# A margin of planned time on what TensorE waits for, in a kernel whose order of work a list scheduler writes

## The chip, the cores and the metric

The kernel runs on one NeuronCore of a Trainium2 chip. The metric is the device time of one execution in microseconds; lower is better. Work is done by TensorE (matrix products into PSUM), VectorE (DVE), ScalarE (ACT) and GpSimd (POOL); SyncE (SP) issues all transfers. Each engine runs its own instructions in the order in which the program gives them and waits on semaphores for the others.

## The reference

Two independent branches on inputs of 2048 x 448, with their results side by side in an output of 2048 x 896.

```python
def _A_ref(x, dft_seq_re, dft_seq_im, dft_hid_re, dft_hid_im):
    a = jnp.einsum("bsd,ed->bse", x, dft_hid_re)
    b = jnp.einsum("bsd,ed->bse", x, dft_hid_im)
    return jnp.einsum("ts,bse->bte", dft_seq_re, a) - jnp.einsum("ts,bse->bte", dft_seq_im, b)

def _B_ref(x, wqkv, wo):
    B, S, D = x.shape            # 1, 2048, 448
    H = 16; Dh = D // H          # 28
    ...
    scores = jnp.einsum("bhqd,bhkd->bhqk", q, k) * Dh ** -0.5
    p = _softmax(scores, axis=-1)
    o = jnp.einsum("bhqk,bhkd->bhqd", p, v)
    return (lambda x, *d: x.transpose(*d))(o, 0, 2, 1, 3).reshape(B, S, D) @ wo
```

## The kernel before

**Work.** Branch A is a Fourier mixing step: 32 tiles of rows of the hidden transform (`hidden`) and then, for 16 tiles of rows and two parts, real and imaginary, 48 products each against the sequence matrices (`sequence`, L558). Every operand is split into a rounded part and a remainder, and three products make up one (`Piece`: ACT rounds a 256 KB piece of the matrix, POOL or at the start DVE subtracts). Branch B makes q and k (`project`) and v (`values`; L458 with `hidden`), then runs attention for 64 units, that is 16 heads and four chunks of 512 queries, and last multiplies by the output matrix (L853).

**Two kinds of unit.** `unit_kept`, three of a head's four chunks, computes 16 score products of 128 keys x 512 queries (L702). ACT, for the second one ACT or DVE, copies each out of its bank (L335, L337) and DVE takes a running maximum in the tile `rm` (L709, L712). Then come four transpositions (L719), a reduction (L721), four transpositions (L728), the subtraction of the maximum on POOL or DVE (L745) and the exponentials on ACT (L749). `unit_twice`, one chunk of each head, computes the scores once for their maxima (L652, with DVE's L656) and again with the maxima as further rows of the product (L680, with ACT's exponentials L684). Its q rows lie in one of two tiles `qr`, which `load_q` fills (L585, L586) when the unit before last has let the tile go. The product with v is issued in groups of eight (`pv_group`, L633; 16 records of the profile), two groups a unit, and `unit_out` copies the result out on ACT or DVE. `head_out` folds the four partial sums of a head (L763) and divides.

**Fill.** The products of L458 and L558 need few results of the other engines. They are spread over the span as fill: their keys (`fkey`) run from 8 to 1120 on the planner's clock, and they use two PSUM banks of their own (`fill_s`). Attention has the other six (`bank_s`).

**The order** is written by a list scheduler on the host, while the program is built. Each piece of work is a `Task` with a key, the engines that may run it with a duration for each, the tasks that it depends on, and the `Slot`s (tiles or banks from a pool of `Slots`) that it uses. `Schedule.run` steps through time. Whenever an engine is idle it looks through that engine's heap of ready tasks in the order of their keys and takes the first whose slots are to be had (`can_take`) and whose locks are free; what can't be taken is set aside for the next look. A task counts as seen by other engines `lat` after its end (0.15, for TensorE 0.25); then its slots go back to their pool and its dependents are woken. Dependents on the same engine are woken at its end (`own`). The planner's durations are constants: 0.2335 and 0.2365 for a product of 512 columns, 0.2065 for one of 448, 0.60 for a DVE step over a bank with `RAW` = 0.16 more between two maxima on one tile, 0.48 for a copy on ACT. After a value group it takes another value group first, if one can be taken, and it counts `PE_TURN` = 0.22 for each turn from other products to one. The order in which tasks are taken is the order of the instructions of each engine; their semaphore waits follow from what they read and write. On the chip nothing knows of the planner's times.

Of the kernel before, what the change touches and what calls it, by code (L numbers as in the profile page):

```python
# [50 lines left out]
RAW = 0.16  # L51
LANES = 8
FLOW = 200.0
PE_TURN = 0.22


class Slot:


    def __init__(self, pool):  # L60
        self.pool, self.i, self.users, self.lock = pool, None, 0, 0.0
        self.key = None
# [6 lines left out]
class Slots:  # L69


    def __init__(self, tiles, in_turn=False):
        self.tiles, self.in_turn = tiles, in_turn
        self.free = list(range(len(tiles)))
        self.turns = []

    def slot(self):
# [1 line left out]
        self.turns.append(s)  # L79
        return s  # L80

    def can_take(self, slots):
        n = len(self.free)
        if n < len(slots):
            return False
        if self.in_turn:
            return all(s in self.turns[:n] for s in slots)
        return True

    def take(self, slot):  # L90
        slot.i = self.free.pop(0)
        self.turns.remove(slot)


class Task:
    __slots__ = ("engs", "key", "emit", "lat", "use", "lock", "left", "then", "mode", "n", "dmas", "own")


class Schedule:
# [26 lines left out]
            self.wake(t)  # L126
        return t

    def wake(self, t):
        for e in t.engs:  # L130
            heapq.heappush(self.ready[e], (t.key, t.n, t))

    def run(self):
        now, events, count = 0.0, [], 0
        for p in self.pools:
            p.turns.sort(key=lambda s: s.key)
        idle = {e: True for e in self.ENGINES}
        mode = 0
        done = set()
        landed, flow = [], 0.0  # L140
        while True:
            for e in self.ENGINES:
                if not idle[e]:
                    continue
                aside, pick, first = [], None, None
                if e == "SP" and len(landed) >= LANES and landed[-LANES] > now + 1e-9:
                    heapq.heappush(events, (landed[-LANES], 2, count, "tick", None))
                    continue
                heap = self.ready[e]
                while heap:  # L150
                    item = heapq.heappop(heap)
                    t = item[2]
                    if t.n in done:
                        continue
                    wants = {}
                    for s in t.use:
                        if s.i is None:
                            wants.setdefault(s.pool, []).append(s)
                    if any(not p.can_take(w) for p, w in wants.items()) or any(x.lock > now + 1e-9 for x in t.lock):
                        aside.append(item)  # L160
                        continue
                    if e == "PE" and mode == 1 and t.mode == 0 and pick is None:
                        if not any(x[2].mode == 1 and x[2].n not in done for x in heap):
                            pick = t
                            break
                        first = first or item
                        aside.append(item)
                        continue
                    pick = t
                    break  # L170
                if pick is None and first:
                    pick = first[2]
                    aside.remove(first)
                for item in aside:
                    heapq.heappush(heap, item)
                if pick is None:
                    continue
                t = pick
                done.add(t.n)
                for s in t.use:  # L180
                    if s.i is None:
                        s.pool.take(s)
                dur = t.engs[e]
                if e == "PE":
                    if t.mode > mode:
                        dur += PE_TURN
                    mode = t.mode
                lat = t.lat
                if e == "SP":

                    at = now
                    for size, extra in t.dmas:
                        if len(landed) >= LANES:
                            at = max(at, landed[-LANES])
                        flow = max(flow, at + 0.4) + size / FLOW
                        landed.append(max(at + 1.35 + size / 170 + extra, flow + 1.1))
                        at += 0.38
                    dur = at - now
                    lat = max(landed[-len(t.dmas):]) - at + 0.1
                t.emit(e)  # L200
                count += 1
                idle[e] = False
                for x in t.lock:
                    x.lock = now + dur + 0.05
                heapq.heappush(events, (now + dur, 0, t.n, "free", (e, t)))
                heapq.heappush(events, (now + dur + t.own, 1, t.n, "own", (e, t)))
                heapq.heappush(events, (now + dur + lat, 1, t.n, "seen", (e, t)))
                if t.lock:
                    heapq.heappush(events, (now + dur + 0.06, 2, t.n, "tick", None))
            if not events:  # L210
                break
            now = self.now = events[0][0]
            while events and events[0][0] <= now + 1e-9:
                _, _, _, what, x = heapq.heappop(events)
                if what == "free":
                    idle[x[0]] = True
                elif what == "own":
                    for n in x[1].then:
                        if x[0] in n.engs and len(n.engs) == 1:
                            n.left -= 1  # L220
                            if n.left == 0:
                                self.wake(n)
                elif what == "seen":
                    e, t = x
                    for s in t.use:
                        s.users -= 1
                        if s.users == 0:
                            s.pool.free.append(s.i)
                    for n in t.then:
                        if e in n.engs and len(n.engs) == 1:  # L230
                            continue
                        n.left -= 1
                        if n.left == 0:
                            self.wake(n)
        assert count == self.n, (count, self.n, now)
        return now

# [661 lines left out]
```

## Time and profile before

| | |
|---|---|
| median of three runs | 1205.03 us (1199.01 to 1207.03) |
| profiled execution | 1200.74 us |
| its span in the profile | 1199.0 us |
| granted clock of TensorE in it | 0.997 |

The profile's engines are PE (matmuls), PEld (weight loads of TensorE, which overlap matmuls), DVE, ACT, POOL and SP; a "q" behind a name is its sequencer. In lists of waits the columns are: engine, tile and line that waited, `<-` what ended the wait, then the total in us, the number of waits and the longest. "issue" stands for waits that nothing in the profile explains. In a timeline each row has the start, the time it took, engine, line, operation, tiles, shape and how many instructions are merged; in square brackets stands the idle time of the engine before it and what ended it. A gap of TensorE is shown where no matmul's record covers it; since the records of successive matmuls overlap, a late start can be covered. A product with v stands as two records (2,048 for 1,024 instructions).

### The profile page before, as it was taken

How to read it: one execution, taken by the hardware profiler on the slowest of the kernel's cores; microseconds unless marked ns; L12 is line 12 of the kernel's file. 1: busy time of each engine (PE TensorE's matmuls, PEld its weight loads, DVE VectorE, ACT ScalarE, POOL GpSimd, SP SyncE). 2: the span in 40 equal slices, each digit the busy share in tenths (PEclk: the TensorE clock that was granted, in tenths of full speed). 3: DMA queues.
4: the chain of work that ended last, by engine and by line, in shares of the span. 5: the costliest groups of instructions: out<-in, count | busy, mean ns of one | idle time of the engine just before them, and what ended most of it. 6: DMA issues, size and time to landing. Idle time of an engine off the chain costs nothing.

```text
span 1199.0 us, 19665 instructions
## 1 busy us (share of the span) xinstructions
PE 1170.1 (98%) x6404; PEld 795.4 (66%) x6404; DVE 919.5 (77%) x1429; ACT 1055.1 (88%) x1768; POOL 949.2 (79%) x567
## 2 busy tenths in 40 slices
PE   7999999999999999999999999999999999999998
PEld 5876666666667666576666666666567666676588
DVE  6599979888788788787888888888768878867301
ACT  4279999999999999898999999999979999999733
POOL 3157777889989789776988799789869888989963
PEclk9999999999999999999999999999999999999999
DMA  8873244332233231323232333233322323223542
GB/s 255 176 189 110 91 141 144 97 81 75 87 87 92 69 99 58 101 74 104 73 104 66 101 98 98 65 88 90 106 87 73 105 82 108 84 72 98 190 151 107
DMA packets 106150, 125.15 MB, mean 104 GB/s; under 512 B 47460, under 2 KB 61412, under 8 KB 104788
## 3 DMA queue, kind: packets, MB, share of 16 engines
q1 hardware_dynamic: 106048, 123.91, 35.5%
q8 instruction: 50, 0.82, 0.3%
q14 instruction: 52, 0.43, 0.1%
HBM read 89.98 MB, written 33.75 MB: 103 GB/s over the span
## 4 chain that ended last, share of the span: by engine, by line
PE 85%; ACT 4%; DMA 4%; DVE 2%; issue 1%; SPq 1%; POOL 1%; DVEq 0%; POOLq 0%; ACTq 0%
PE bank L558 23%; PE bank L633 17%; PE bank L702 14%; PE bank L458 13%; PE bank L652 5%; PE bank L680 5%; PE bank L853 3%; DMA qr<-qkd 2%; PE bank L719 2%; ACT kept L335 2%; PE bank L728 2%; DVE rm L712 2%; ACT kept L749 1%; PE bank L763 1%; DMA sm<-kept 0%
## 5 line engine op out<-in xcount | busy, mean ns | idle before, releaser
L745 POOL TENSOR_TENSOR kept<-kept,mb 128x1024 f32<-128x1024 f32 x280 | 667.2, 2404 | 76.7 <-ACT mb L730 54.4
L712 DVE TENSOR_TENSOR rm<-bank,rm 128x512 f32<-128x512 f32 x672 | 461.1, 686 | 68.0 <-PE bank L702 21.7
L335 ACT ACTIVATE kept<-bank 128x512 f32<-128x512 f32 (+1 forms) x736 | 414.6, 620 | 63.1 <-PE bank L702 39.0
L749 ACT ACTIVATE kept<-kept 128x1024 f32<-128x1024 f32 x384 | 401.1, 1081 | 13.4 <-POOL kept L745 7.7
L558 PE MATMUL bank<-big,whi 128*128 128x448 f32 x1024 | 324.1, 370 | 0.0
L702 PE MATMUL bank<-qk,k 84*128 84x512 f32 x768 | 292.3, 414 | 1.6 <-DVE rm L712 0.9
L434 POOL TENSOR_TENSOR wlo<-wraw,whi 128x512 fp32r<-128x512 f32 (+1 forms) x166 | 203.7, 1230 | 95.4 <-ACT whi L429 60.1
L633 PE MATMUL bank<-kept,v 128*32 128x512 f32 x2048 | 243.8, 597 | 1.2 <-ACT kept L749 0.8
L558 PEld LDWEIGHTS bank<-big,whi 128*128 128x128 f32 x1024 | 193.2, 190 | 29.5 <-issue 7.5
L656 DVE TENSOR_REDUCE mx<-bank 128x1 f32<-128x512 f32 x256 | 173.5, 683 | 31.4 <-PE bank L652 30.3
L702 PEld LDWEIGHTS bank<-qk,k 84*128 84x128 f32 x768 | 141.5, 189 | 80.6 <-DVE rm L712 22.5
L558 PE MATMUL bank<-big,wlo 128*128 128x448 f32 x512 | 189.1, 369 | 0.4 <-POOL wlo L434 0.4
L684 ACT ACTIVATE kept<-bank 128x512 f32<-128x512 f32 x256 | 155.4, 617 | 4.8 <-PE bank L680 4.3
L633 PEld LDWEIGHTS bank<-kept,v 128*32 128x32 f32 x2048 | 56.0, 109 | 124.4 <-issue 110.1
L745 DVE TENSOR_TENSOR kept<-kept,bank 128x1024 f32<-128x1024 f32 x104 | 125.8, 1212 | 7.0 <-ACT mb L730 6.5
L429 ACT ACTIVATE whi<-wraw 128x512 fp32r<-128x512 f32 x167 | 108.1, 648 | 13.8 <-PE bank L558 6.2
L652 PE MATMUL bank<-k,qr 84*128 84x512 f32 x256 | 104.1, 417 | 12.3 <-DMA qr<-qkd 8.4
L558 PEld LDWEIGHTS bank<-big,wlo 128*128 128x128 f32 x512 | 97.0, 190 | 14.8 <-issue 2.5
L680 PE MATMUL bank<-qr,k 86*128 86x512 f32 x256 | 104.6, 415 | 0.0
L337 DVE COPY kept<-bank 128x512 f32<-128x512 f32 (+1 forms) x48 | 32.7, 682 | 61.9 <-PE bank L702 29.2
L458 PE MATMUL bank<-big,whi 128*128 128x512 f32 x196 | 71.9, 411 | 6.8 <-ACT big L396 5.3
L652 PEld LDWEIGHTS bank<-k,qr 84*128 84x128 f32 x256 | 47.7, 190 | 43.4 <-DVE rm L712 11.3
(80 smaller groups left out, 1065.9 us busy)
## 6 DMA issues: line engine op xcount, KB each, us to landing
wraw<-wre SPq DMA_DIRECT2D x64, 256.0 KB
wraw<-wim SPq DMA_DIRECT2D x64, 256.0 KB
wraw<-xa SPq DMA_DIRECT2D x32, 256.0 KB
out<-kept SPq DMA_DIRECT2D x32, 224.0 KB
k<-qkd SPq DMA_DIRECT2D x15, 448.0 KB
qkd<-kept SPq DMA_DIRECT2D x24, 256.0 KB
qk<-qkd SPq DMA_DIRECT2D x48, 112.0 KB
qkd<-wdh SPq DMA_DIRECT2D x17, 256.0 KB
```

Source lines behind the costliest of these rows:

```text
L335: nc.scalar.activation(dst, src, AF.Copy)
L434: b = sch.add(e, key + 1.5, lambda g: eng[g].tensor_tensor(self.lo.t[:, :n], raw.t[:, :n], f32(self.hi.t)[:, :n], op=ALU.subtract), deps=[ ...
L458: nc.tensor.matmul(o.t[:, :cols], w(), x(), start=(i == 0), stop=(i == n - 1))
L558: nc.tensor.matmul(o.t[:, :D], a.t[:, k, :], b[:, q * 4 + k, :], start=(q == 0 and k == 0 and j == 0), stop=(q == 3 and k == 3 and j == 2))
L633: nc.tensor.matmul(o.t[j * VW:(j + 1) * VW, :], VT[h].t[:, kt // 4, j, :], pairs[i // 2].t[:, i % 2, :], start=(kt < 4), stop=(kt >= NT - 4))
L652: m = pe(key, lambda e, o=o, kc=kc, qt=qt: nc.tensor.matmul(o.t, q.t[:KR, qt * P:(qt + 1) * P], KT[h].t[:KR, kc * CH:(kc + 1) * CH], start ...
L656: ms.append(dve(key - 20, lambda o=o, kc=kc, qt=qt: nc.vector.tensor_reduce(mx.t[:, qt, kc:kc + 1], o.t, axis=AX.X, op=ALU.max), deps=[m], ...
L680: m = pe(key, lambda e, o=o, kt=kt: nc.tensor.matmul(o.t, KT[h].t[:KR + 2, kt * P:(kt + 1) * P], q.t[:KR + 2, :], start=True, stop=True), ...
L702: m = pe(key, lambda e, o=o, kt=kt: nc.tensor.matmul(o.t, KT[h].t[:KR, kt * P:(kt + 1) * P], q.t[:KR, :], start=True, stop=True), deps=[*l ...
L712: prev = dve(key - 20, lambda o=o: nc.vector.tensor_tensor(rm.t, o.t, rm.t, op=ALU.max), deps=[m, prev], use=[rm, o], lock=[o], own=RAW)
L745: eng[e].tensor_tensor(s.t, s.t, over_pair(pm.t if e == "DVE" else mb.t), op=ALU.add)
L749: es.append(act(key, lambda s=s: nc.scalar.activation(s.t, s.t, AF.Exp, scale=SCALE), 0.96, deps=[sh], use=[s]))
```

## The change

The planner takes a task on TensorE only if everything it waits for has been there for 0.15 us of planned time. A pool now keeps with each free tile the time since when it is free, and a task the time at which its last dependency was seen. For tasks on TensorE both must lie at least `AHEAD` = 0.15 before now; for the other engines the margin is zero. A task that is woken by one on its own engine, or has no dependency, has the stamp -1 and passes. Until the margin has passed the planner sees the next ready task in the order of keys, which may be fill. A further event 0.15 after each task has been seen makes the planner look again. No task, duration, key, tile or pool is changed.

```diff
+AHEAD = 0.15
...
-        self.free = list(range(len(tiles)))
+        self.free = [(i, -1.0) for i in range(len(tiles))]
...
-    def can_take(self, slots):
-        n = len(self.free)
+    def can_take(self, slots, before):
+        n = sum(since <= before for _, since in self.free)
         if n < len(slots):
             return False
...
-        slot.i = self.free.pop(0)
+        slot.i = self.free.pop(0)[0]
...
-    def wake(self, t):
+    def wake(self, t, since=-1.0):
+        t.since = since
         for e in t.engs:
             heapq.heappush(self.ready[e], (t.key, t.n, t))
...
                 heap = self.ready[e]
+                before = now - (AHEAD if e == "PE" else 0.0) + 1e-9
                 while heap:
...
-                    if any(not p.can_take(w) for p, w in wants.items()) or any(x.lock > now + 1e-9 for x in t.lock):
+                    if t.since > before or any(not p.can_take(w, before) for p, w in wants.items()) or any(
+                            x.lock > now + 1e-9 for x in t.lock):
                         aside.append(item)
                         continue
...
-                            s.pool.free.append(s.i)
+                            s.pool.free.append((s.i, now))
...
-                            self.wake(n)
+                            self.wake(n, now)
+                    heapq.heappush(events, (now + AHEAD, 2, t.n, "tick", None))
```

More of the change, by code (lines that the diff above doesn't have):

```diff
@@ L90, in take @@
     def take(self, slot):
-        slot.i = self.free.pop(0)
+        slot.i = self.free.pop(0)[0]
         self.turns.remove(slot)
 class Task:
-    __slots__ = ("engs", "key", "emit", "lat", "use", "lock", "left", "then", "mode", "n", "dmas", "own")
+    __slots__ = ("engs", "key", "emit", "lat", "use", "lock", "left", "then", "mode", "n", "dmas", "own", "since")
 class Schedule:
```

## The prediction

> **What bounds the kernel now.** I read the page first: the busy times, then the chain that ended last.
>
> ```profile
> span 1199.0 us, 19665 instructions
> ...
> PE 1170.1 (98%) x6404; PEld 795.4 (66%) x6404; DVE 919.5 (77%) x1429; ACT 1055.1 (88%) x1768; POOL 949.2 (79%) x567
> ...
> PE 85%; ACT 4%; DMA 4%; DVE 2%; issue 1%; SPq 1%; POOL 1%; DVEq 0%; POOLq 0%; ACTq 0%
> ```
>
> TensorE carries 85% of the chain and shows 1199.0 - 1170.1 = 28.9 us of idle time. That is not all it loses: a matmul's record overlaps the next one's, so a product that starts 0.1 us late leaves no gap. I therefore priced a stream without delays from start to start, with the longest undisturbed piece of the chain, one of its long value groups, and three places of the timeline of TensorE.
>
> ```profile
> 258.57 3.57 PE bank L633 x32
> ...
> 1158.64 26.75 PE bank L853 x132
> ```
>
> ```profile
> 202.17 0.40 PE L458 MATMUL bank<-big,wlo 128*128 128x512 f32 x1
> 202.50 1.92 PE L633 MATMUL bank<-kept,v 128*32 128x512 f32 x16
> 204.35 0.50 PE L702 MATMUL bank<-qk,k 84*128 84x512 f32 x1
> 204.69 0.40 PE L458 MATMUL bank<-big,whi 128*128 128x512 f32 x1
> ...
> 206.32 0.40 PE L458 MATMUL bank<-big,whi 128*128 128x512 f32 x1
> ```
>
> ```profile
> 234.07 1.06 PE L763 MATMUL bank<-ou,fold 128*32 128x512 f32 x8
> 234.95 1.90 PE L633 MATMUL bank<-kept,v 128*32 128x512 f32 x16
> ...
> 241.04 0.60 PE L719 MATMUL bank<-ident,rm 128*128 128x128 f32 x4
> 241.40 0.50 PE L680 MATMUL bank<-qr,k 86*128 86x512 f32 x1
> 241.75 0.40 PE L652 MATMUL bank<-k,qr 84*128 84x512 f32 x1
> ```
>
> A product of 448 columns takes 26.75 / 132 = 0.203 us. One of 512 takes (206.32 - 204.69) / 7 = 0.233 us, seven starts lying between those two rows. A value group of 16 records takes 204.35 - 202.50 = 1.85 us, two joined ones 3.57. The step into a group is 0.33 and the one after it 0.34, together 0.20 us over two plain steps. Four transpositions take 0.36 and the step after them 0.35, so 0.48 us over a plain stream. Folding a head takes 0.88 us. The loops of the code give the counts: 2,240 products of 448 columns, 1,588 of 512, 128 value groups (in 111 stretches as the program stands, 17 of them joined), 96 sets of transpositions, 16 heads. The sum is 454 + 370 + (94 x 1.85 + 17 x 3.57) 235 + 111 x 0.20 = 22 + 96 x 0.48 = 46 + 16 x 0.88 = 14, in all 1141 us. So 1199 - 1141 = 58 us are lost, 29 in gaps that are shown and 29 in delays too short to show (2 ns on each of 3,828 spacings would move that by 8).
>
> The waits of TensorE's matmuls and of its weight loads tell where:
>
> ```profile
> PE bank L652 <- DMA qr<-qkd: 8.4, 7, 2.6
> PE bank L458 <- ACT big L396: 5.3, 1, 5.3
> PE bank L652 <- DVE rm L712: 2.6, 4, 1.2
> ```
>
> ```profile
> PEld bank L702 <- DVE rm L712: 22.5, 54, 1.0
> PEld bank L652 <- DVE rm L712: 11.3, 19, 1.6
> ...
> PEld bank L680 <- DVE rm L712: 10.0, 24, 0.8
> ...
> PEld bank L702 <- DVE kept L745: 6.1, 8, 0.8
> ...
> PEld bank L702 <- DVE mx L656: 4.3, 13, 0.8
> ...
> PEld bank L702 <- ACT kept L684: 4.2, 15, 0.9
> ...
> PEld bank L652 <- ACT kept L684: 2.1, 10, 0.3
> ...
> PEld bank L702 <- DVE rm L709: 1.8, 10, 0.3
> ```
>
> (us in total, times, longest.) The long waits are transfers at the head of a unit and the start of the kernel. The many short ones are score products whose bank an ACT or DVE instruction was still reading. The timeline shows what one costs:
>
> ```profile
> 317.56 0.69 DVE L712 TENSOR_TENSOR rm<-bank,rm 128x512 f32<-128x512 f32 x1 [0.46 <-ACT kept L335]
> 317.69 0.57 PE L558 MATMUL bank<-big,whi 128*128 128x448 f32 x2
> ...
> 318.30 0.19 PEld L702 LDWEIGHTS bank<-qk,k 84*128 84x128 f32 x1 [0.42 <-DVE rm L712]
> 318.31 0.50 PE L702 MATMUL bank<-qk,k 84*128 84x512 f32 x1
> ...
> 318.41 0.19 PEld L558 LDWEIGHTS bank<-big,wlo 128*128 128x128 f32 x1
> ...
> 318.64 0.37 PE L558 MATMUL bank<-big,wlo 128*128 128x448 f32 x1
> ```
>
> The product of L702 was due at 317.69 + 2 x 0.203 = 318.10 and came at 318.31. The next came 0.33 later instead of 0.233, since its own weight load had to follow the late one. The wait cost 0.21 + 0.10 us.
>
> **The change part by part.** The stamps on free tiles and on tasks, the two new arguments and the extra ticks are work of the planner on the host; no instruction comes of them, and their cost on the chip is nothing. What reaches the chip is the order. The program as built has the same 5,316 products, and its score products, value groups and fill products stand within some tens of places of where they stood, from first to last: neither stream is run down earlier, so no tail is added and no TensorE work is added or removed.
>
> *The cushion.* The planner took a product the moment that it held the bank to be free; now it lets it be free for 0.15 us and takes a fill product meanwhile. On the chip the late load finds its semaphore up to 0.15 us earlier in TensorE's order. Upper end: the 54 + 19 + 24 = 97 waits for a running maximum, each 0.15, give 14.6 us; the 56 of the other five rows, at most about 0.1 us each, as after the example's late load, give 5.6; together 20 us. It can't be the whole 58: the 8.4 and the 5.3 are transfers and the start, and 0.15 each is 1.2 of them. Lower end: nothing, if the lag is one of rate. For that speaks the maximum, a chain on one tile:
>
> ```profile
> 318.17 0.68 DVE L656 TENSOR_REDUCE mx<-bank 128x1 f32<-128x512 f32 x1
> 318.76 1.48 DVE L712 TENSOR_TENSOR rm<-bank,rm 128x512 f32<-128x512 f32 x2
> 320.16 0.68 DVE L656 TENSOR_REDUCE mx<-bank 128x1 f32<-128x512 f32 x1
> ```
>
> An unchained DVE step takes 0.59 us (318.17 to 318.76), the two chained ones 1.40, so the second 0.80. The planner's constants give it 0.60 + 0.16 = 0.76. Every chained maximum puts DVE 0.04 us behind the plan, and a cushion of 0.15 is used up after about four, until DVE next runs dry. And the 97 waits left the load idle for 43.8 / 97 = 0.45 us on average, more than 0.15. I take the middle of 0 and 20: 10 us. A gain below zero in this term I exclude, as a longer distance in the order can't make a bank come free later.
>
> *What is late next.* ACT, with DVE behind it:
>
> ```profile
> 100.00:1125.00 1025.00, 1009.56 (x5639) 665.42 (x5638) 838.38 (x1276) 972.91 (x1622) 865.63 (x486) 1.00 0.32 92
> ```
>
> ```profile
> L335 ACT ACTIVATE kept<-bank 128x512 f32<-128x512 f32 (+1 forms) x736 | 414.6, 620 | 63.1 <-PE bank L702 39.0
> ```
>
> In the attention stage (columns: PE, PEld, DVE, ACT, POOL) ACT is busy 973 of 1025 us, so 10 us less leaves it 42 us of room and 20 us less 32. Seven copies of a unit's output go from DVE to ACT in the new order: 7 x 414.6 / 736 = 3.9 us of ACT, hidden in those 52 us of idle time and worth 3.9 us if they were not.
>
> *Moved by the way.* Value groups now stand in 107 stretches, 21 of them joined: 4 x (2 x 1.85 - 3.57 + 0.20) = 1.3 us less. The q rows of a unit that computes its scores twice are fetched into one of two tiles which a unit before frees: in the built order the work of TensorE between the product that lets the fetch go and the first that needs it is, by the spacings above, 6.3, 6.3, 6.4, 6.8, 6.9, 7.0 and 7.2 us for the seven shortest before and 6.2, 6.2, 6.4, 6.5, 6.6, 6.6 and 6.8 after, together 1.6 us less, and seven is the number of waits in the row of 8.4 us. So 1.6 us come back there. Nothing is put into SP's queue or taken from it; its transfers only change places by a few.
>
> Sum: -10 - 1.3 + 1.6 = -9.7 us, against the profiled execution's 1200.74 us (span 1199.0): 1191. That execution lies 4.3 us below the median of the three runs, 1205.03; the same share, 0.8%, off the median gives 1195.3. I say 1196.
>
> **The Trainium skill against the trace.** In the rows at 318.30 the load of the fill product, which waited for no result, began 0.11 us after the late load and not before it. The Trainium skill, "TensorE: Matmul & The Clock Gate", section "Step-by-step: what each phase is for", says that TensorE's queue pulls weight loads ahead of matmuls in flight; a queue that did so past a waiting load would have this load done by 318.31, and the 0.10 us behind each late load would not exist. By that rule the five short rows hold nothing to win, and the term falls from 10 to about 7 us; this trace speaks against it.
>
> **The rivals.** *The cushion covers everything short.* For it: the lag of the example, 0.21 us, is not much over 0.15, and fill products without waits stand ready all the time. Against it: the mean idle of 0.45 us and the chained maxima. It gives the upper 20 us: 1200.7 - 20 - 0 = 1181, which in the measure of the median is 1185. Chance 0.27.
>
> *It does nothing measurable*, though the order differs: DVE and ACT run behind by rate, and a product put 0.15 us later waits for the next result instead. For it: ACT's 95% and the 0.04 us per maximum. Against it: TensorE, not they, carries 85% of the chain. It gives 1200.7 + 1.6 - 1.3 = 1201, so 1205. Chance 0.17. By the rule of the skill the result would lie between this and my forecast.
>
> *Slower, by the fetch of the q rows.* The new order has shortened this cover, and the reshuffle may put a store of DMA ahead of a fetch in SP's queue. In the row of 8.4 us seven units waited, the worst 2.6 us. If all 16 units waited 2.6, that would be 41.6 - 8.4 = 33 us more; with no gain from the cushion 1234, or 1238 by the median. It decides from 10 us more, where it has eaten the gain, and makes the kernel slower by over 1% from 12 + 10 = 22 us more, 1.9 us at each unit. Against it: the cover is 0.2 us shorter, not 2. Chance 0.09.
>
> **How the numbers follow.** The partial cushion has the remaining 0.47, its own range 1187 to 1203. About 1% is what a measurement of this kernel can tell from no change, so "faster" ends at 1193. Faster is the full cushion, 0.27, and the low tail of my case, 0.06: 0.33. Slower is the last rival: 0.09. The rest, 0.58, lies within. The range reaches down to 1184, which leaves out part of the full cushion, and up to 1210, which holds the third case with the spread of the three runs (1199 to 1207) and leaves out the slow one.
>
> **What would show it.** Right: the weight loads' waits for a running maximum fall from 97 and 43.8 us to about 60 and 25; TensorE's busy time falls by 7 to 10 us at the same number of records, its listed idle time stays near 29; the wait for q rows stays between 7 and 12 us; ACT's share in the attention stage rises from 95 to 96%. The full cushion would show nearly none of the waits for maxima. The third case would show them as many as before, behind other products. Wrong altogether: a wait for transfers above 20 us, or ACT and DVE with idle time that a product of TensorE ended and that has grown by as much as the waits have fallen.

## The result and the profile after

The changed kernel is slower by 0.6%: 1208.21 us median of 19 runs (1205.15 to 1213.60) against 1201.76 us of 19 runs of the kernel before, ratio 1.0059 with a 95% interval of 1.0047 to 1.0071. The forecast was 1196 us, 0.8% faster.

Line numbers after the new constant are one higher, and from the scheduler on five higher: L702 is now L707, L652 is L657, L680 is L685, L712 is L717. The page of the changed kernel:

```profile
span 1207.5 us, 19649 instructions
...
PE 1173.8 (97%) x6404; PEld 804.7 (67%) x6404; DVE 914.0 (76%) x1426; ACT 1056.5 (87%) x1774; POOL 947.7 (78%) x564
...
PE 78%; DMA 7%; ACT 6%; DVE 4%; issue 3%; POOL 1%; SPq 1%; DVEq 0%; POOLq 0%; ACTq 0%
```

TensorE carries 78% of the chain instead of 85%, with DMA, ACT and DVE in its place. Its idle time that shows has grown from 28.9 to 1207.5 - 1173.8 = 33.7 us. The waits of its matmuls and of its weight loads:

```profile
PE bank L657 <- DMA qr<-qkd: 7.8, 7, 1.7
PE bank L463 <- ACT big L401: 5.3, 1, 5.3
PE bank L707 <- ACT kept L689: 2.5, 3, 1.6
PE bank L724 <- DVE rm L717: 2.4, 1, 2.4
PE bank L685 <- DMA qr<-nmd: 2.3, 1, 2.3
```

```profile
PEld bank L707 <- DVE rm L717: 19.2, 40, 1.5
...
PEld bank L685 <- DVE rm L717: 12.5, 22, 2.7
PEld bank L657 <- DVE rm L717: 11.6, 17, 2.3
```

The waits for a running maximum have become fewer, 40 + 22 + 17 = 79 instead of 97, but they take 43.3 us instead of 43.8, and the longest is 2.7 us where 1.6 was the longest. Three rows have come up to near the top: ACT's exponentials, a maximum at a set of transpositions, and the round trip of a unit's maxima through DRAM (`qr<-nmd`).

To see the small delays too I took, for each pair of successive starts on TensorE, the time over the lower quartile that the kernel before has for the same pair of lines (a product after a value group or a set of transpositions as a case of its own), from 40 us on. The same count, with the same quartiles, was made for each run of the table; the start of a product at half clock counts as late. The two columns behind the ratio set the end of TensorE's work in the planner's own time, and the span of the profile, against the kernel before.

| profiled run | margin, us | median ratio | planned end of TensorE, us | span, us | delays of 30 to 150 ns, us | 150 to 600 ns | over 600 ns | us at half clock |
|---|---|---|---|---|---|---|---|---|
| before | 0 | 1 | 0 | 0 | 17.1 | 6.9 | 12.3 | 6.8 |
| changed | 0.15 | 1.0059 | +6.4 | +8.5 | 15.5 | 13.6 | 18.6 | 10.4 |
| turn 0.23 | 0 | 1.0157 | +7.7 | +18.0 | 18.9 | 17.0 | 18.2 | 23.9 |
| turn 0.23 | 0.15 | 1.0100 | +8.6 | +13.2 | 13.0 | 20.3 | 21.3 | 20.9 |
| turn 0.21 | 0 | 1.0075 | -2.2 | +11.1 | 15.0 | 9.7 | 22.4 | 20.5 |
| turn 0.21 | 0.15 | 1.0085 | +8.3 | +10.2 | 12.7 | 10.4 | 23.2 | 13.7 |
| margin 0.02 | 0.02 | 1.0128 | -1.0 | +12.6 | 14.9 | 14.3 | 23.0 | 23.9 |
| margin 0.30 | 0.30 | 1.0177 | +27.7 | +24.8 | 12.3 | 27.3 | 20.4 | 34.1 |
| maxima 0.20 | 0 | 1.0227 | +7.2 | +28.4 | 15.9 | 16.8 | 32.3 | 32.1 |
| exchange 0.15 | in the order alone | 1.0008 | 0 | +4.1 | 17.2 | 9.3 | 13.7 | 10.2 |
| exchange 0.30 | in the order alone | 1.0048 | 0 | +8.2 | 18.2 | 12.0 | 13.6 | 10.4 |

In the changed kernel the short delays are 1.6 us less and those over 150 ns are 13.0 us more. The sum, 11.4 us, stands beside 8.5 us of span.

The planned times come from the kernels themselves: `Schedule.run` gives them on the host, and the order that it writes is the one in which TensorE, DVE, ACT and SP ran in the trace. They show what the margin costs before anything runs. In the plan before, TensorE's work ends at 1167.9 us, with 24.6 us of idle time; in the changed plan at 1174.3, with 31.7. Idle time in a plan is time in which the planner had nothing that it could take; the end moves a little less than the idle time because the changed plan counts fewer turns. The wait of 2.4 us for a maximum at L724, listed above, stands in the plan with 2.42 us. The trace follows the plan, though not closely: at the same amount of work done, the changed plan is behind the plan before by 2.5 us after 300 us of TensorE's planned work, 2.7 after 900, 5.6 after 1000 and 6.4 at the end, and the changed trace behind the trace before by 1.5, 5.1, 6.3 and 8.5.

One new delay that the plan does not have, in the timelines of SP and of TensorE of the changed kernel:

```profile
934.61 0.54 SPq L591 DMA_DIRECT2D k<-qkd  x1
935.27 0.26 SPq L673 DMA_DIRECT2D nmd<-n  x1
940.16 0.23 SPq L674 DMA_DIRECT2D qr<-nmd  x1
```

```profile
938.60 0.73 PE L707 MATMUL bank<-qk,k 84*128 84x512 f32 x2
941.60 0.77 PE L685 MATMUL bank<-qr,k 86*128 86x512 f32 x1 [2.26 <-DMA qr<-nmd]
942.16 0.63 PE L707 MATMUL bank<-qk,k 84*128 84x512 f32 x1
942.59 0.57 PE L563 MATMUL bank<-big,wlo 128*128 128x448 f32 x1
```

The keys of a head were fetched just ahead of the store of a unit's maxima; store and load then took 940.16 - 935.27 = 4.9 us, SP waited through it, and TensorE stood still for 2.26 us. The starts after it are 0.43 us apart where a product takes 0.233: the clock had been halved. The windows around it (columns from the third: PE, PEld, DVE, ACT, POOL, then the granted clock), and those around the one such place in the kernel before:

```profile
930.00:941.10 11.10, 9.34 (x58) 5.07 (x56) 8.56 (x15) 10.46 (x18) 11.10 (x7) 1.00 0.32 76
941.10:947.90 6.80, 6.30 (x18) 5.45 (x19) 2.07 (x3) 3.15 (x5) 2.37 (x2) 0.50 0.63 190
```

```profile
867.90:874.70 6.80, 6.40 (x20) 5.37 (x21) 3.52 (x6) 2.31 (x4) 0.67 (x1) 0.50 0.24 87
```

So this wait is paid twice: 2.26 us of it, and half of the 6.8 us after it. Not every wait of its length is. In the same trace this one was followed by no time at half clock:

```profile
1120.11 0.66 PE L724 MATMUL bank<-ident,rm 128*128 128x128 f32 x4 [2.37 <-DVE rm L717]
```

### The profile page after: what moved, and what is told of

Its sections match the earlier page's. It is cut to its first block, busy times and chain, and to the rows that moved or that the text cites. A ratio compares the mean times of both kernels' runs of the same rounds, so it can differ in the third digit from the quotient of the medians.

```text
span 1207.5 us, 19649 instructions
## 1 busy us (share of the span) xinstructions
PE 1173.8 (97%) x6404; PEld 804.7 (67%) x6404; DVE 914.0 (76%) x1426; ACT 1056.5 (87%) x1774; POOL 947.7 (78%) x564
## 4 chain that ended last, share of the span: by engine, by line
PE 78%; DMA 7%; ACT 6%; DVE 4%; issue 3%; POOL 1%; SPq 1%; DVEq 0%; POOLq 0%; ACTq 0%
PE bank L563 20%; PE bank L638 16%; PE bank L707 13%; PE bank L463 13%; PE bank L657 5%; PE bank L685 4%; PE bank L858 3%; DVE rm L717 3%; DMA qr<-qkd 3%; ACT kept L340 2%; PE bank L724 2%; PE bank L733 2%; ACT kept L754 2%; POOL kept L750 1%; ACT kept L689 1%
## 5 line engine op out<-in xcount | busy, mean ns | idle before, releaser
L717 DVE TENSOR_TENSOR rm<-bank,rm 128x512 f32<-128x512 f32 x672 | 461.1, 686 | 89.3 <-PE bank L707 33.1
L340 ACT ACTIVATE kept<-bank 128x512 f32<-128x512 f32 (+1 forms) x735 | 420.3, 634 | 57.3 <-PE bank L707 33.8
L754 ACT ACTIVATE kept<-kept 128x1024 f32<-128x1024 f32 x384 | 408.1, 1106 | 14.9 <-POOL kept L750 11.7
L707 PE MATMUL bank<-qk,k 84*128 84x512 f32 x768 | 292.8, 413 | 4.3 <-ACT kept L689 2.5
L707 PEld LDWEIGHTS bank<-qk,k 84*128 84x128 f32 x768 | 141.3, 189 | 78.8 <-DVE rm L717 19.2
L689 ACT ACTIVATE kept<-bank 128x512 f32<-128x512 f32 x256 | 160.1, 638 | 10.8 <-PE bank L685 9.7
L434 ACT ACTIVATE whi<-wraw 128x512 fp32r<-128x512 f32 x167 | 112.7, 675 | 12.3 <-DMA wraw<-wim 7.4
L657 PE MATMUL bank<-k,qr 84*128 84x512 f32 x256 | 103.3, 416 | 8.4 <-DMA qr<-qkd 7.8
L685 PE MATMUL bank<-qr,k 86*128 86x512 f32 x256 | 105.3, 417 | 5.2 <-DMA qr<-nmd 2.3
L657 PEld LDWEIGHTS bank<-k,qr 84*128 84x128 f32 x256 | 47.9, 191 | 35.6 <-DVE rm L717 11.6
```

Source lines behind the costliest of these rows:

```text
L340: nc.scalar.activation(dst, src, AF.Copy)
L657: m = pe(key, lambda e, o=o, kc=kc, qt=qt: nc.tensor.matmul(o.t, q.t[:KR, qt * P:(qt + 1) * P], KT[h].t[:KR, kc * CH:(kc + 1) * CH], start ...
L689: es.append(act(key - 20, lambda o=o, p=p: nc.scalar.activation(p.t, o.t, AF.Exp, scale=SCALE), deps=[m], use=[o, p.pair]))
L707: m = pe(key, lambda e, o=o, kt=kt: nc.tensor.matmul(o.t, KT[h].t[:KR, kt * P:(kt + 1) * P], q.t[:KR, :], start=True, stop=True), deps=[*l ...
L717: prev = dve(key - 20, lambda o=o: nc.vector.tensor_tensor(rm.t, o.t, rm.t, op=ALU.max), deps=[m, prev], use=[rm, o], lock=[o], own=RAW)
L754: es.append(act(key, lambda s=s: nc.scalar.activation(s.t, s.t, AF.Exp, scale=SCALE), 0.96, deps=[sh], use=[s]))
```

## The experiments

Two theories stood against each other. **M**: the margin costs by itself, as attention's products come later. **L**: any new order of this list schedule is a new draw, and the order before was a good one; the margin itself moves little. A third, **H**, was added: the margin helps by some 5 us, under an even larger loss by the draw.

**A new order without a margin.** `PE_TURN = 0.22` becomes 0.23 in the kernel before.

> No margin at all; the planner's constant for a turn to a value group is 0.23 instead of 0.22, which parts the order of TensorE from that of the kernel before after 403 products. Theory L (a new order is a new draw, and the order before was a good one): ratio 1.003 to 1.010, delays over 0.15 us in the attention stage near the 31 us of the changed kernel rather than the 19 us of the kernel before. Theory M (the margin itself costs, by taking attention's products later): ratio 0.998 to 1.002 and delays near 19 us.

Ratio 1.0157 (1.0134 to 1.0179): slower than the change itself, with no margin anywhere. It lies outside both ranges: far from M's 0.998 to 1.002, and over L's upper end of 1.010. Its delays over 150 ns are 35.2 us. Its plan ends 7.7 us later (some 1.2 us of it are the constant itself, 0.01 at each of about 119 turns), and the span is 18.0 us longer.

**A margin too short to cover anything.** `AHEAD = 0.02`.

> The margin is 0.02 us, too short to cover a late result, and the order is new. Theory L: ratio 1.003 to 1.010, as any other order. Theory M: the cost goes with the margin, so ratio 0.999 to 1.002.

Ratio 1.0128 (1.0108 to 1.0149), outside both ranges again. The cost on the chip does not go with the margin; the planned end of this order is even 1.0 us earlier.

**Twice the margin.** `AHEAD = 0.3`.

> The margin is 0.30 us, twice that of the change. Theory M: the cost doubles, ratio 1.009 to 1.015. Theory L: the cost has nothing to do with the margin, ratio 1.000 to 1.010, with results that come late by 0.05 to 0.2 us rarer still than the 109 of the changed kernel (175 before).

Ratio 1.0177 (1.0155 to 1.0200), the worst of the three margins and over what either theory allowed. Its short delays are the lowest of the table, 12.3 us, and its delays of 150 to 600 ns the highest, 27.3 us. In planned time the margin does cost by its size: the end moves by -1.0, 6.4 and 27.7 us with 0.02, 0.15 and 0.30. At 0.30 the whole loss of span, 24.8 us, is less than that.

**A truer constant for DVE.** `RAW = 0.16` becomes 0.2, with no margin; the trace before had shown 0.80 us for a chained maximum where the planner had 0.76.

> No margin; the planner's time between two chained maxima is 0.20 instead of 0.16 over the step, so 0.80 as the trace shows it. If the long delays come of DVE falling behind the plan by rate, they shrink: the waits for a running maximum fall by a third and the ratio is 0.992 to 0.998. Theory L: the better constant is lost in the draw, ratio 1.000 to 1.010.

Ratio 1.0227 (1.0196 to 1.0258). The constant that fits the chip better gave a much worse order, outside both ranges, with a plan 7.2 us longer and a span 28.4 us longer. If DVE's lag by rate matters, this run does not show it.

**Partners with and without the margin.** To part the margin from the draw, the margin of 0.15 was set to the turn constant 0.23, and a second pair was made at 0.21.

> The change's margin of 0.15 us with the planner's turn constant at 0.23: the partner of the run at 0.23 without a margin, which had the ratio 1.016. Theory L (the order is a draw, the margin itself moves little): anywhere from 1.005 to 1.023, whatever the partner had. Theory M (the margin costs 0.6% by itself): 1.019 to 1.025. A third, H (the margin helps by some 5 us, and the order before was an unusually good draw): below the partner, 1.008 to 1.014.

> No margin, the turn constant at 0.21: another order without a margin. Theory L and H: slower than before, ratio 1.008 to 1.022, with three to eight stretches of half clock against one. Theory M: 0.998 to 1.002, and the run at 0.23 was an accident.

> The margin of 0.15 with the turn constant at 0.21: partner of the run at 0.21 without one. Theory L: between 1.005 and 1.023, on either side of its partner. Theory M: 0.004 to 0.008 above its partner. Theory H: 0.003 to 0.008 below it.

At 0.23 the margin's kernel is below its partner (1.0100, 1.0082 to 1.0118, against 1.0157), at 0.21 a little above (1.0085, 1.0064 to 1.0105, against 1.0075, 1.0060 to 1.0090), at the original 0.22 above (1.0059 against 1). The run at 0.21 without a margin lies just under the range of L and H and far from M's. The means of the three are 1.0081 with the margin and 1.0077 without: no side. M's fixed cost is refuted and H is not borne out; the draws spread over 1.6%, and the order before is the best of them.

Against the plan the pairs look different. The margin moves the planned end by 6.4, 0.9 and 10.5 us (at 0.22, 0.23 and 0.21) and the span by 8.5, -4.8 and -0.9. Beyond its plan the chip loses, compared with the kernel before, 4.6 us with the margin and 10.3 without at 0.23, and 1.9 and 13.3 at 0.21; at 0.22 it is 2.1 and, by definition, 0. The delays of 30 to 150 ns fall in all three pairs, by 1.6, 5.9 and 2.3 us. This fits a cushion that does work and is paid for with a longer plan, which the means then hide. It is not shown: each number is one order, and the order before needed no margin to keep to its plan.

**Three tiles for the q rows.** No margin; the pool `qr` has 3 tiles and `NKEPT` is 18, to test whether the waits at the head of a unit make the difference.

> No margin; three tiles for the q rows of a unit that computes its scores twice instead of two, and 18 pairs kept instead of 19 to make room. It is a new order too. If the waits for q rows are what most long waits are and what brings the half clock, the row of the wait for q rows falls from 8.4 to under 2 us, there are at most two stretches of half clock, and the ratio is 0.993 to 1.005. If long waits turn up elsewhere in any new order: ratio 1.008 to 1.020 and four or more stretches.

Ratio 1.0322 (1.0296 to 1.0347), the worst run of all and over both ranges. The wait for q rows left the top of the list, and another wait took its place:

```profile
PE bank L652 <- DMA k<-qkd: 16.2, 12, 3.1
```

The keys of a head are needed by the same products as the q rows; in these twelve waits they landed 5.1 to 7.7 us after their issue. The plan of this order ends 15.4 us later than that of the kernel before, so the run does not test the q rows alone.

**The margin without a new draw.** The planner runs as before, with no margin, and every engine but TensorE gets its order to the letter. Where TensorE takes a score product whose bank or result has been free for less than 0.15 us of planned time, and its next task is a fill product, the two are written in the other order. That is the margin's act, with no new plan following from it, at 409 of the 692 places where this plan takes a task of TensorE inside the margin; 546 of the 692 are score products, the others mostly value groups and transpositions.

```diff
...
-                t.emit(e)
+                if e == "PE":
+                    if held and (dur not in FILLS or t in held.then):
+                        held.emit("PE")
+                        held = None
+                    if dur == 0.2365 and max(fresh) > now - AHEAD:
+                        held = t
+                    else:
+                        t.emit(e)
+                        if held:
+                            held.emit("PE")
+                            held = None
+                else:
+                    t.emit(e)
...
```

(`fresh` has the stamps of the task and of the banks that it takes; `FILLS` the durations of fill products.)

> The plan of the kernel before, with no margin in it; but where TensorE takes a score product whose bank or result has been free for less than 0.15 us of planned time and its next task is a fill product, the two are written in the other order. 409 such pairs; ACT, DVE, POOL and SP keep the order of before to the letter. This is the margin without a new draw. If the cushion works as forecast (5 to 10 us of the short delays): ratio 0.990 to 0.997, with delays of 30 to 150 ns falling from 17 us to under 13 and long waits as before, one stretch of half clock. If the margin does nothing by itself: 0.998 to 1.002. If the margin harms by itself, because score products come later: 1.003 to 1.008.

> The same with 0.30 us: 635 pairs exchanged. Cushion: a little below the run with 0.15, 0.988 to 0.996. Nothing: 0.998 to 1.002. Harm: 1.004 to 1.010.

> Control: the exchange is made for 148 score products whose bank and result had been free for at least 0.30 us, and for no other. Cushion and nothing: 0.998 to 1.003, since nothing of these was late. Harm by taking score products later: 1.001 to 1.004.

With 0.15 the ratio is 1.0008 (0.9995 to 1.0021): nothing. With 0.30 it is 1.0048 (1.0030 to 1.0066): harm. The control, 148 exchanges of products that were not late, gives 1.0013 (1.0002 to 1.0024), which lies in both of its ranges: an exchange that can gain nothing may cost a little, and what the 409 exchanges gained and what they cost are measured only together. The exchange did reach the late results: weight loads of score products in the attention stage whose result came 50 to 200 ns after the previous product's start were 175 before, 129 with 0.15 and 110 with 0.30 (109 in the changed kernel). Yet delays of 30 to 150 ns stayed at 17.2 and 18.2 us against 17.1. One wait of a reader for TensorE grew, that of DVE's reduction of the scores; here it is in the kernel before, with 0.15 and with 0.30 (L680 on L676 are L656 on L652 there):

```profile
DVE mx L656 <- PE bank L652: 30.3, 28, 4.3
```

```profile
DVE mx L680 <- PE bank L676: 34.1, 37, 4.0
```

```profile
DVE mx L680 <- PE bank L676: 35.6, 39, 4.2
```

The readers as a whole waited hardly longer: from 100 to 1125 us all of DVE's waits for TensorE take 123.4, 122.5 and 124.1 us (118, 126 and 129 of them), and ACT's 37.3, 37.2 and 40.8.

**The q fetch told to the planner.** `load_q` gets 2.0 us more of planned landing time in `unit_twice`.

> No margin; the planner is told that the fetch of the q rows of a unit that computes its scores twice lands 2.0 us later, about what the worst waits for it were. A new order again, with two tiles as before. If the long waits of a draw are transfers that land later than planned, the row of the wait for q rows falls from 8.4 to under 3 us and nothing takes its place: at most two stretches of half clock, ratio 0.990 to 1.003. If a new order finds other long waits whatever is mended: the row falls all the same, and the ratio is 1.005 to 1.016, with four or more stretches.

The built order came out the same in every place on every engine, so this was a second run of the kernel before: ratio 0.9994 (0.9977 to 1.0010). The plan already had the rows in time, since 2.0 us more changed nothing in it. On the chip six of the seven waits of the kernel before are for rows that were issued right behind the keys of a head and landed 4.4 to 6.2 us after their issue. As a control the run shows two things: a ratio of 0.9994 comes of the same program, and in its profiled run no time after the first 40 us was at half clock, against 6.8 us in that of the same program before. So the time at half clock differs by a few microseconds between executions of one program.

**The collision in SP's queue.** In the traces the store and load of a unit's maxima take 1.3 us where nothing lies ahead and mostly 4.2 to 5.2 us where the keys of a head were fetched just before. Over 2.5 us take 6 of 16 before, 9 after, 7 to 9 in the seven other orders of the table that come of a new plan. The edit takes the order as planned and moves only the fetch of the keys behind that round trip, if it is among the next three of SP; the other engines' order stays to the letter. It moves the keys of seven heads in the changed kernel and of six in the kernel before.

```diff
+            near = [i for i in sp[:3] if row[i][1] in self.stores]
+            if near:
+                to = next(i for i in sp if i > near[0] and row[i][1] in self.loads)
...
+                    row.insert(to, row.pop(at))
```

> The changed kernel, margin 0.15 and all; only in SP's queue the load of a head's keys goes behind the next store and load of a unit's maxima, where these are among the next three. If the collisions are what the new order lost: round trips over 2.5 us fall from 9 to at most 2, the wait of 2.3 us for maxima and its stretch of half clock go, and the ratio falls from 1.006 to 0.998 to 1.002. If they only go with it, since the keys land later instead and are needed at once: the waits for q rows or keys grow by as much, ratio 1.003 to 1.010.

> The same edit in the kernel before. If the collisions cost: ratio 0.993 to 0.998, with round trips over 2.5 us falling from 6 to at most 2. If the keys are needed at once: 1.000 to 1.006.

The round trips shortened as meant (2 over 2.5 us in the changed kernel, none in the other), the wait of 2.3 us for maxima went, and both kernels became much slower, beyond either forecast: 1.0211 (1.0184 to 1.0238) and 1.0126 (1.0099 to 1.0153). The waits of TensorE in the edited changed kernel and in the edited kernel before:

```profile
PE bank L673 <- DMA k<-qkd: 15.1, 5, 3.5
PE bank L673 <- DMA qr<-qkd: 8.2, 4, 3.1
```

```profile
PE bank L668 <- DMA k<-qkd: 12.6, 4, 5.0
...
PE bank L668 <- DMA qr<-qkd: 4.7, 3, 2.0
```

Those two runs added 1.5% and 1.3% by the place of seven and six fetches of keys in SP's queue. Undoing the collisions in this way costs more than they do, since the keys are then late; what the collisions themselves cost is not parted from that.

No version beat the kernel before.

## Why the prediction was wrong

**What bounds the kernel** was read rightly: TensorE in a stream without delays, and some 58 us lost, half of it out of sight. The mechanism of a late load, too: a result that comes 0.2 us late costs the product and the weight load behind it.

**The cushion is the step that failed.** The prediction took 10 us from between 0 and 20 and excluded a gain below zero, "as a longer distance in the order can't make a bank come free later". The exchange measured it in the old plan, at 409 places: 0.0008, so about 1 us worse, with an interval from 0.6 us better to 2.5 us worse; at 0.30 us it is 5.8 us worse. One account is a ring of bank, product and reader: a product written one place later runs later, its DVE or ACT reader with it, and the bank that this reader frees, for which a product further down waits. It is not shown: one row of reader waits grew from 28 to 37 and 39, but DVE's waits for TensorE as a whole did not grow in time, and no product was traced around the ring. The rival that gave the cushion no effect had the right size for this step in the old plan; its reason, that DVE and ACT run behind by rate, no run shows.

**The price of the margin in the plan was put at nothing.** The prediction let the planner take "a fill product meanwhile" and costed the new order at 1.6 - 1.3 = 0.3 us, since products, value groups and fill stand "within some tens of places" of where they stood. There is not always a fill product to take: the plan itself leaves TensorE idle 7.1 us longer and ends its work 6.4 us later. The medians lie 1208.21 - 1201.76 = 6.5 us apart. Of the changed kernel's 0.6%, then, the exchange accounts for about 0.1%, and the rest came only with the new plan, whose longer end is as large as the whole loss. That the two sizes agree so well is in part luck, as the runs stand: measured against the kernel before, the other orders of the table that come of a new plan lost from 1.9 to 21.2 us of span beyond their plans, and the one with 0.30 lost 2.9 less than its plan. The delays over 150 ns in the attention stage spread over many causes: against the kernel before, those ended by a running maximum rose from 4.9 to 9.0 us, by the exponentials of a second pass from 1.4 to 5.1, by the round trip of maxima from nothing to 2.4, by the q fetch from 7.7 to 8.1. I found no single place behind it. What stays open is why the chip keeps to some of these plans and falls 10 to 21 us behind others, and whether the margin helps there.

**The number** hides the miss: 1208 lies inside the stated range of 1184 to 1210. That is luck. The range reached over no change and beyond, and it was laid around a median of three runs, 1205.03, that is 3.3 us above the median of 19.

**The q fetch** stayed between the 7 and 12 us that were named, but 1.6 us more was expected and the row says 7.8 against 8.4. **The slower rival** had the wrong place: fetches at the head of each unit did not go to 2.6 us, and in the changed kernel the longest is 1.7. **ACT** was not next: its busy time is 1056.5 us against 1055.1, and in the attention stage 967 of 1025 us against 973, so its share fell where a rise from 95 to 96% had been named.

**The signs that the prediction named** told it apart: waits for maxima fell in number (97 to 79, where about 60 had been named) and not in time (43.8 to 43.3, where 25 had), and TensorE's busy time rose by 3.7 us where 7 to 10 less had been named.

**The rule of the Trainium skill** on weight loads pulled ahead of matmuls ("TensorE: Matmul & The Clock Gate", "Step-by-step: what each phase is for") would have made the term smaller, and the result came out smaller still, but not by that rule: in the trace after, too, the fill product's load behind a load that waited for a running maximum starts 0.11 us after it at the earliest, in 53 cases. The page speaks of matmuls in flight and not of a load that waits.

## What to carry to other kernels

A rule in a list scheduler is first judged by the scheduler's own clock: where its plan ends, and how long the engine that bounds the kernel stands idle in it. That needs no chip, and here it names a loss of the size that was measured. It is not the whole: the order is also one draw from many that look alike, and what the chip loses beyond the plan differs by tens of microseconds from one to the next. So compare a rule over several draws (a constant moved by 0.01 makes one), with and without it, or write it into the finished order at the places where it acts and leave the rest to the letter. A product that is taken later has a reader that is later, too, so a margin is not free.

## What the runs showed of the hardware

The clock of TensorE can fall to half after waits that are shorter than I had thought to matter: in the changed kernel the clock fell at 941.1 us, while TensorE stood still for 2.26 us until 941.6, and stayed at 0.50 for 6.8 us, as in the window rows above. After the first 40 us, and but for the last one at the end of a span, the stretches in all runs last 3.4 or 6.8 us. The Trainium skill, "TensorE: Matmul & The Clock Gate", section "What's actually happening", gives a window of about 3.4 us for this gate and half clock after an idle one; the length of the stretches agrees with it, while here a wait of two thirds of a window was followed by half clock. The length of the wait does not decide alone: the wait of 2.37 us at 1120.1, and one of 2.56 us in the kernel before that ended at 486.6, were followed by none, and one of 1.44 us in the changed kernel that ended at 807.6 was, for 3.4 us.

Time at half clock after the first 40 us runs from none to 34.7 us over the profiled runs. It is 6.8 us before and 10.4 us after, and half of the difference is 1.8 us. Over all runs it is more: the mean granted clock is 0.9971 in the 73 runs of the kernel before that stand beside the experiments and 0.9946 in the 19 of the changed kernel, which makes 3.5 and 6.5 us of lost clock. By this estimate up to 3 us of the change's 6.5 us pass through the clock.
